# The first feed-forward product by Strassen's method, two tiles at a time, from tile 8 on

## The chip, the cores and the metric

The kernel runs on one core of a Trainium2 chip. The metric is the device time in microseconds of one execution. The engines are named as in the profile: PE is the matrix engine (PEld its weight loads), DVE, ACT and POOL are the vector, scalar and general-purpose engines, and SP issues the DMAs. PE reads its operands from SBUF and writes into PSUM banks of 128 partitions by 512 float32.

## The reference

Banded attention of 8 batches, 8 heads, 576 positions and 64 features per head, then a normalized feed-forward layer of width 512 to 2048 to 512 with a residual:

```python
# heads 0..3: the last 32 keys; heads 4..7: every 4th of the last 128 keys
scores = np.where(masks[None, :, :, :], scale * np.matmul(q, k.transpose(0, 1, 3, 2)), -1000000000.0)
attn = np.exp(scores - np.max(scores, axis=-1, keepdims=True))
attn = attn / (np.sum(attn, axis=-1, keepdims=True) + 1e-09)
x = np.matmul(attn, v).transpose(0, 2, 1, 3).reshape(B, S, H * D)  # (8, 576, 512)
xn = (x - mu) / np.sqrt(var + 1e-06) * g_ln
out = x + np.maximum(xn @ w_ch1, 0.0) @ w_ch2
```

The weights come as float64, everything else as float32.

## The kernel before

The 4608 rows are 36 tiles (`NT`) of 128 rows. Attention is computed a tile at a time: L loads q, k and v, A (`attn_prep`) splits them into float16 halves, S (`attn_scores`) makes the two sets of scores on PE and masks them on DVE, M (`attn_softmax`) makes the softmax on DVE, POOL and ACT and turns the probabilities round by 32-square DVE transposes (`to_columns`), V (`attn_values`) multiplies by the values on PE and leaves the tile's result `x`. N (`norm`) normalizes `x` and splits it into a high and a low float16 half, `xh` and `xl` (L568, L569); T (`transposes`) turns both round by two DMA transposes issued from SP (L576). Tiles 0 to 3 (`EARLY`) take another route through attention, in float32, while the weights are still being loaded and converted.

Every float32 product of the feed-forward is made of three float16 products: high by high, high by low, low by high. The first product, "up" (`up`, L597), has 128 by 128 pieces of `w_ch1` as the stationary operand and the transposed `x` as the moving one. Per chunk of 128 hidden features that is 4 pieces of the depth of 512, times 3, 12 matmuls. ACT takes the relu of the bank as the high half `hh` (L603), and DVE makes the low half `hl` (L604). The second product, "down" (`down`, L620), has 128-column pieces of `hh` and `hl` as the stationary operand and 512 columns of `w_ch2` as the moving one, 48 matmuls a tile, cut into four parts of 12. After the fourth, DVE adds the residual (L626) and SP stores the tile.

Blocks are of `NB` = 3 tiles. The first two blocks (`APART`) run up a tile at a time, with 128 moving columns; from tile 6 on, up has 384 moving columns for three tiles at once, 192 matmuls a block. There are two copies of the transposed `x` (`xT`), used in turns, so that T of a block may run while up of the block before it still reads.

The order of work is a list of units with due times: `unit` gives each its time, not earlier than those of the units it names as having to come first, and the list, sorted by time, is the order in which the program is written down. From there the framework orders the instructions of each engine along a simulated time line (`schedule_with_timeline_sim=True`); those inside `tc.high_priority()` go ahead of others that are ready. At run time each engine goes through its own list in order. For tiles that are not early, the due time of A is `start - AHEAD - PER_TILE * ...`, where `start` is when the block's up is due. `MOVED` puts single units at other times by hand. In each pool, a buffer is given out again once its last reader is done: `ps_f` has 4 banks, `slot` has `SLOTS` = 5 buffers (raw weights, q and k of every other tile, and the split q and k of each tile).

Of the kernel before, what the change touches and what calls it, by code (L numbers as in the profile page):

```python
# [32 lines left out]
NBLK = NT // NB  # L33
EARLY = 4
AHEAD = 64.3
GAP = 17.2
SOFTMAX, VALUES, READY = 0.9, 23.0, 21.7
LOAD = -12.6
PER_TILE = 21.7
CW, SLOTS = 2, 5  # L40
HG = 4
SUMS = 128
# [6 lines left out]
    "U": (42.0, 66.0, 84.0), "D": 106.0, "v": 70.0, "X": 84.0, "t": (88.0, 112.0),  # L49
# [9 lines left out]
}  # L59
APART = 2  # L60
# [8 lines left out]
def attention_then_ffn(ctx: ExitStack, tc, qkv, masks, g, w1, w2, out):  # L69
# [33 lines left out]
    for i in range(NV):  # L103
# [4 lines left out]
    w1_sb = const.tile([P, NKC + 1, NKC, DM], F32, name="w1_sb")  # L108
    w1_16 = w1_sb.bitcast(F16).rearrange("p q c (a f) -> p q c a f", a=2)
    xT = [  # L110
        const.tile([P, 2, NKC, NB * P], F16, name="xT"),
        w1_16[:, NKC].rearrange("p c a f -> p (c a f)")[:, 0 : 2 * NKC * NB * P].rearrange(
            "p (a c n) -> p a c n", a=2, c=NKC
        ),
    ]


    w2_sb = const.tile([P, NFC, DM], F32, name="w2_sb")
    def w2_f32(f, n):
        x, at = (w2_sb, f + 4) if f < NFC - 4 else (w1_sb[:, NKC], f - NFC + 4)  # L120
        return x[:, at : at + n]
# [3 lines left out]


# [43 lines left out]
    def load_tile_now(t):  # L170
        if t == 0:
            state["early"] = work.tile([P, 2, 2, HP, P], F32, name="qk32", bufs=1)
# [4 lines left out]
        else:  # L177


            if t % 2:  # L180
                qk32 = slot().bitcast(F32).rearrange("p (a x h c) -> p a x h c", a=2, x=2, h=HP)
            else:
                qk32 = work.tile([P, 2, 2, HP, P], F32, name="qk32", bufs=1)
# [70 lines left out]
    def room_of(t):  # L254

        st = state[t]
        x = slot().bitcast(F16)
        at = 0
        for name, *shape in (("qs", H, P), ("khp", HP, W + P), ("klp", HP, W + P), ("khd", HP, P), ("kld", HP, P), ("vl", H, D)):
            n = shape[0] * shape[1]  # L260
            st[name] = x[:, at : at + n].rearrange("p (h c) -> p h c", h=shape[0])
            at += n

# [197 lines left out]
    def values_early(t):  # L461
# [21 lines left out]
        x = work.tile([P, 2, HP, D], F32, name="x", bufs=2 * NB + 1)  # L483
# [47 lines left out]
    def to_x(t, pv, scale):  # L531
# [7 lines left out]
        x = work.tile([P, 2, HP, D], F32, name="x", bufs=2 * NB + 1)  # L539
# [5 lines left out]
    def norm(t):  # L545
# [9 lines left out]
        xn = work.tile([P, DM], F32, name="xn", bufs=1)  # L555
# [10 lines left out]
        xh = work.tile([P, DM], F16, name="xh")  # L566
        xl = work.tile([P, DM], F16, name="xl")
        nc.scalar.copy(xh, xn)  # L568
        nc.gpsimd.tensor_tensor(out=xl, in0=xn, in1=xh, op=ALU.subtract)  # L569
        st.update(xh=xh, xl=xl)  # L570

    def transposes(t, blk, i):
        st = state[t]
        blk["xTh"], blk["xTl"] = xT[blk["b"] % 2][:, 0], xT[blk["b"] % 2][:, 1]
        for name, src in (("xTh", st["xh"]), ("xTl", st["xl"])):
            nc.sync.dma_start_transpose(out=blk[name][:, :, i * P : (i + 1) * P], in_=src)  # L576


    def ffn(blk, apart):

        n = NB
        hs = [None] * (NFC // HG)

        def up(fs, i0, i1):

            cols = slice(i0 * P, i1 * P)
            z = ps_f.tile([P, 512], F32, name="ps_f")
            z = z[:, 0 : len(fs) * (i1 - i0) * P].rearrange("p (f n) -> p f n", f=len(fs))
            for n, f in enumerate(fs):
                fq, fc = f // 4, slice(f % 4 * P, (f % 4 + 1) * P)  # L590
# [322 lines left out]
```

## Time and profile before

| | |
|---|---|
| time, median of 3 runs | 942.48 us (940.19 to 942.51) |
| span of the profiled execution, first to last instruction | 942.2 us |
| mean granted PE clock over the span | 0.985 |
| first up (tile 0) | at 58.3 us |
| last matmul of tile 5's up, the last with 128 moving columns | at 231.2 us |
| last block: down of tiles 30 to 32, up, and down of tiles 33 to 35 | 844.99 to 938.36 us |

The page gives the span of the profiled execution and no separate time for it; the span is 0.3 us from the median of the timed runs. The last three entries are starts of matmuls in the trace. The lines of the profile stand in the prediction, each where it is used. In a line of groups, "x1152 | 345.0, 380" means 1152 instructions, 345.0 us of the engine's time in total and 380 ns from start to end of one; matmuls overlap, so their rate is read from the starts of a run of them, or from the chain of work that ended last, which cuts overlapping pieces at the next one's start.

### The profile page before, as it was taken

To read this page: it belongs to the slowest core of one execution; us is meant where nothing else is said; L and a number is where in the kernel's file an instruction comes from. 1 tells how busy PE (TensorE), PEld (TensorE's weight loads), DVE (VectorE), ACT (ScalarE), POOL (GpSimd) and SP (SyncE) were. 2 spreads that over 40 slices of the span, in tenths; PEclk is the share of its full clock that TensorE was granted. 3 is DMA by queue.
4 is the path that set the end of the run, shared out by engine and by line. 5 is a ranking of instruction groups with operands and counts; after the bars stand their busy time and mean duration, and the time that the engine had idled before them with its cause. 6 is when DMAs were issued, how large, how long until landed. Compare 5 with 4: busy or idle time off the path is not lost.

```text
span 942.2 us, 18610 instructions
## 1 busy us (share of the span) xinstructions
PE 890.7 (95%) x7608; PEld 552.2 (59%) x7608; DVE 634.2 (67%) x1379; ACT 312.7 (33%) x588; POOL 312.3 (33%) x319
## 2 busy tenths in 40 slices
PE   4479789999999999999999999999999999999998
PEld 4379466777665555565565565565565565564553
DVE  4799658896977577786686686686686685660210
ACT  4556742334323343251241451241241341130110
POOL 1010273646234235454253353354243341120000
PEclk9979899999999999999999999999999999999999
DMA  7887872754344516446143654364043411010000
GB/s 241 311 229 229 187 176 50 153 122 115 66 75 93 148 52 133 92 71 136 37 80 71 169 105 71 89 123 90 30 88 69 87 27 37 21 24 23 12 1 34
DMA packets 79622, 93.39 MB, mean 99 GB/s; under 512 B 47920, under 2 KB 53680, under 8 KB 79536
## 3 DMA queue, kind: packets, MB, share of 16 engines
q1 hardware_dynamic: 79536, 92.21, 42.3%
q8 instruction: 59, 0.97, 0.4%
q14 instruction: 27, 0.22, 0.1%
HBM read 71.86 MB, written 9.44 MB: 86 GB/s over the span
## 4 chain that ended last, share of the span: by engine, by line
PE 81%; DMA 10%; ACT 3%; DVE 3%; issue 2%; SPq 1%; POOL 1%; ACTq 0%; DVEq 0%; POOLq 0%
PE ps_f L597 36%; PE ps_f L620 35%; PE ps_s L330 4%; PE ps_v L528 4%; DMA row<-in_qkv 4%; DMA slot<-in_w 3%; DMA xT<-xl 1%; ACT row L226 1%; DMA slot<-in_qkv 1%; DMA v<-in_qkv 0%; PE ps_f L673 0%; ACT w_sb L153 0%; DVE slot L662 0%; POOL slot L280 0%; DVE slot L154 0%
## 5 line engine op out<-in xcount | busy, mean ns | idle before, releaser
L620 PE MATMUL ps_f<-w_sb,hh 128*128 128x512 f16 x1152 | 345.0, 380 | 5.8 <-ACT w_sb L153 5.0
L597 PEld LDWEIGHTS <-w_sb 128*128 128x128 f16 x3072 | 256.0, 99 | 126.6 <-issue 4.6
L620 PE MATMUL ps_f<-w_sb,hl 128*128 128x512 f16 x576 | 219.1, 380 | 0.0
L597 PE MATMUL ps_f<-xT,w_sb 128*128 128x384 f16 (+1 forms) x1536 | 199.2, 289 | 2.9 <-DMA xT<-xh 2.4
L597 PE MATMUL ps_f<-w_sb 128*128 128x384 f16 (+1 forms) x1536 | 196.7, 287 | 0.0
L620 PEld LDWEIGHTS <-hh 128*128 128x128 f16 x1152 | 111.8, 98 | 131.5 <-issue 6.8
L603 ACT ACTIVATE hh<-ps_f 128x384 f16<-128x384 f32 (+1 forms) x184 | 91.1, 500 | 216.8 <-PE ps_f L597 216.8
L604 DVE SCALAR_TENSOR_TENSOR hl<-ps_f,hh 128x384 f16<-128x384 f32 (+1 forms) x184 | 100.2, 569 | 42.4 <-ACT hh L603 40.3
L620 PEld LDWEIGHTS <-hl 128*128 128x128 f16 x576 | 56.5, 98 | 67.1 <-issue 1.8
L362 DVE TENSOR_TENSOR sc<-ps_s,mask 32x256 f32<-32x256 f32 x128 | 53.6, 419 | 51.2 <-PE ps_s L330 49.8
L435 DVE STREAM_TRANSPOSE pt_d<-pk 32x256 f32<-32x256 f32 x128 | 79.4, 621 | 1.8
L626 DVE SCALAR_TENSOR_TENSOR row<-ps_f,s,x 128x512 f32<-128x512 f32 x36 | 27.0, 749 | 74.5 <-PE ps_f L620 74.0
L446 POOL TENSOR_TENSOR sc<-sc,mx 128x512 f32<-128x512 f32 x32 | 33.4, 1043 | 116.3 <-DVE mx L444 116.3
L451 ACT ACTIVATE p<-sc 128x512 f32<-128x512 f32 x32 | 20.2, 631 | 128.2 <-POOL sc L446 128.2
L569 POOL TENSOR_TENSOR xl<-xn,xh 128x512 f16<-128x512 f32 x36 | 42.0, 1166 | 59.1 <-ACT xh L568 49.8
L330 PE MATMUL ps_s<-slot 128*128 128x128 f16 (+1 forms) x768 | 58.8, 226 | 2.1 <-DVE sc L348 2.1
L330 PEld LDWEIGHTS <-slot 128*128 128x128 f16 x768 | 50.9, 99 | 12.7 <-DVE sc L348 3.0
L287 POOL COPY slot<-slot 128x128 f16<-128x128 f16 x56 | 17.5, 340 | 119.4 <-PE ps_v L528 119.3
L348 DVE TENSOR_TENSOR sc<-ps_s,mask 32x256 f32<-32x256 f32 x128 | 53.5, 418 | 4.9 <-PE ps_s L330 3.4
L453 POOL TENSOR_TENSOR pk<-p,pk 128x512 f16<-128x512 f32 x32 | 40.7, 1271 | 45.8 <-ACT pk L452 45.8
L458 DVE STREAM_TRANSPOSE pt_b<-pk 32x128 f16<-32x128 f16 x87 | 26.1, 300 | 42.0 <-ACT pk L452 28.4
L554 POOL TENSOR_TENSOR rstd<-rstd,mhalf 128x1 f32<-128x1 f32 x36 | 21.1, 587 | 94.9 <-DVE rstd L553 85.2
(100 smaller groups left out, 961.3 us busy)
## 6 DMA issues: line engine op xcount, KB each, us to landing
qk<-in_qkv SPq DMA_DIRECT2D x36, 512.0 KB, 6.9
slot<-in_qkv SPq DMA_DIRECT2D x32, 512.0 KB, 6.7
slot<-in_w SPq DMA_DIRECT2D x14, 1024.0 KB, 6.3
out_x<-row SPq DMA_DIRECT2D x36, 256.0 KB, 2.0
row<-in_qkv SPq DMA_DIRECT2D x33, 256.0 KB, 2.9
v<-in_qkv SPq DMA_DIRECT2D x33, 256.0 KB, 3.0
slot<-in_w SPq DMA_DIRECT2D x4, 512.0 KB, 7.3
slot<-in_qkv SPq DMA_DIRECT2D x28, 64.0 KB, 4.5
```

The lines of the kernel that those rows point to most:

```text
L330: nc.tensor.matmul(out, lhs, rhs, start=(n == 0), stop=(n == len(terms) - 1))
L348: nc.vector.tensor_tensor(out=sc[pj, 0:HP, :], in0=ps[pj, :, W * j : W * j + 2 * W], in1=mask_16[pj, m : m + 1, :].broadcast_to([W, HP, 2 ...
L362: nc.vector.tensor_tensor(out=sc[pj, HP:H, :].rearrange("p h (t i) -> p h t i", t=2), in0=ps[pj].rearrange("p h (t c) -> p h t c", t=2)[:, ...
L435: nc.vector.transpose(dd[pj].rearrange("p t h (i r) -> p r t h i", r=DIL)[:, j], pk[pj, HP:H, :].rearrange("p h (t i) -> p t h i", t=2),)
L446: nc.gpsimd.tensor_tensor(out=sm, in0=sc, in1=mx.broadcast_to([P, H, 2 * W]), op=ALU.subtract)
L453: nc.gpsimd.tensor_tensor(out=pk16[:, :, :, 1], in0=p32, in1=pk16[:, :, :, 0], op=ALU.subtract)
L528: nc.tensor.matmul(oo, l, r, start=(n == 0), stop=(n == len(mm) - 1))
L569: nc.gpsimd.tensor_tensor(out=xl, in0=xn, in1=xh, op=ALU.subtract)
L597: nc.tensor.matmul(z[:, n], l, r, start=(m == 0), stop=(m == len(mm) - 1))
L603: nc.scalar.activation(hh, z, AF.Relu)
L604: nc.vector.scalar_tensor_tensor(out=hl, in0=z, scalar=0.0, in1=hh, op0=ALU.max, op1=ALU.subtract)
L620: nc.tensor.matmul(o, l, r, start=(f == 0 and m == 0), stop=(f == NFC - 1 and m == 2))
```

## The change

From tile 8 (`FIRST`) on, tiles go in pairs. The pair's normalized `x` (256 rows by 512) is cut into quarters: A11 and A12 are the two halves of the depth of the first tile, A21 and A22 of the second. Four sums of quarters are made on POOL at the end of N of the second tile: S3 = A11 - A21, S1 = A21 + A22, S2 = S1 - A11, S4 = A12 - S2. The weights' quarters (256 of depth by 256 of 512 features, for each of the four groups `fg`) are combined once into T1 to T4 (`combine`), on POOL and for T3 on DVE; T4 takes the place of the quarter B12, after tile 7's up. Up of a pair is then seven products of quarters instead of eight, in two halves `s` of the hidden features. Each product is 24 matmuls with 128 moving columns. Products 6, 7 and 4 are added by PE into the bank `u` that holds product 1, product 3 into the bank `f` that holds product 5; the values in between that another result needs are copied out to SBUF by ACT (`copied`) or added to such a copy by DVE (`added`). The relu halves are made as before, two of the four in each half with the low part on POOL.

Tiles 6 and 7 run up a tile at a time, as tiles 0 to 5 do. There is one copy of the transposed `x` and its sums for the pairs, so that T of a pair comes after the last up step of the pair before it, `(4, 1)`; N of a tile comes after T of the tile before. Of the `ORDER` of a pair, a bracket is a product and its half, a string a part of a down ("p3" is the last part of the tile before). The early tiles' q and k, one in four of the raw weights, and some of the float32 weights move into `tw_sb`, where T1 to T3 are put later; q and k of the other tiles go into `slot`, of which there are 4. The lists of hidden halves (`h`) have 12 buffers that are also used for the copies and for `combine`.

```diff
-AHEAD = 64.3
-GAP = 17.2
+FIRST = 8
+KQ = 256
+AHEAD = 58.0
+GAP = 16.5
-PER_TILE = 21.7
-CW, SLOTS = 2, 5
+PER_TILE = 20.7
+CW, SLOTS = 2, 4
+NH = 12
+NX = 5
...
+    xT = const.tile([P, 2 * 7 * 2 * P], F16, name="xT")
+    xT_pair = xT.rearrange("p (a q k n) -> p a q k n", a=2, q=7, k=2)
...
+            add, sub = ALU.add, ALU.subtract
+            for to, x0, x1, op in ((4, 2, 3, add), (5, 4, 0, sub), (1, 1, 5, sub), (2, 0, 2, sub)):
+                nc.gpsimd.tensor_tensor(out=xs[:, to], in0=xs[:, x0], in1=xs[:, x1], op=op)
+            st.update(halves_for_transpose(xs[:, 1:6], 1))
...
+    def evacuate(z, h, on_pool=False):
+        hh, hl = (h[:, a].rearrange("p g n -> p (g n)") for a in range(2))
+        with tc.high_priority():
+            nc.scalar.activation(hh, z, AF.Relu)
+            if on_pool:
+                nc.gpsimd.tensor_scalar(z, z, scalar1=0.0, scalar2=None, op0=ALU.max)
+                nc.gpsimd.tensor_tensor(out=hl, in0=z, in1=hh, op=ALU.subtract)
+            else:
+                nc.vector.scalar_tensor_tensor(out=hl, in0=z, scalar=0.0, in1=hh, op0=ALU.max, op1=ALU.subtract)
...
+        z = f32_tile().rearrange("p (c f) -> p c f", c=2)
+        e = nc.vector if op in ("T3",) else nc.gpsimd
+        e.tensor_tensor(out=z, in0=pieces(x, 0, fg), in1=pieces(y, 0, fg), op=sub)
+        e.tensor_tensor(out=z, in0=z, in1=pieces(x, 1, fg), op=add)
+        e.tensor_tensor(out=z, in0=z, in1=pieces(y, 1, fg), op=sub)
+        hi, lo = pieces(op, 0, fg), pieces(op, 1, fg)
+        nc.scalar.copy(hi, z)
+        e.tensor_tensor(out=lo, in0=z, in1=hi, op=sub)
...
+    PRODUCTS = {
+        1: ("A11", "11"), 2: ("A12", "21"), 3: ("S4", "22"), 4: ("A22", "T4"), 5: ("S1", "T1"), 6: ("S2", "T2"),
+        7: ("S3", "T3"),
+    }
+    def product(n, s, to, start):
+        x, w = PRODUCTS[n]
+        q = QUARTER[x]
+        for j in range(HG):
+            fg, fc = 2 * s + j // 2, slice(j % 2 * P, (j % 2 + 1) * P)
+            for k in range(2):
+                ws = [pieces(w, a, fg)[:, k, fc] for a in range(2)]
+                for m, (l, r) in enumerate(triple(ws, (xT_pair[:, 0, q, k], xT_pair[:, 1, q, k]))):
+                    nc.tensor.matmul(
+                        to[:, j * P : (j + 1) * P], l, r, start=start and j == 0 and k == 0 and m == 0,
+                        stop=j == HG - 1 and k == 1 and m == 2, skip_group_check=not start,
+                    )
...
+        if n == 1:
+            me["u"] = bank()
+            product(1, s, me["u"], True)
+            me["p1"] = copied(me["u"])
+        elif n == 5:
+            me["f"] = bank()
+            product(5, s, me["f"], True)
+            me["p5"] = copied(me["f"])
+        elif n == 6:
+            product(6, s, me["u"], False)
+            me["u2"] = copied(me["u"])
+        elif n == 2:
+            e = bank()
+            product(2, s, e, True)
+            evacuate(added(e, me["p1"]), outcome(0, 0))
+        elif n == 3:
+            product(3, s, me["f"], False)
+            evacuate(added(me["f"], me["u2"]), outcome(0, 1), True)
+        elif n == 7:
+            product(7, s, me["u"], False)
+            evacuate(added(me["u"], me["p5"]), outcome(1, 1), True)
+        else:
+            product(4, s, me["u"], False)
+            evacuate(me["u"], outcome(1, 0))
...
+        do("N", VALUES + 2, norm, f"V{t}", f"T{t - 1}")
+        unit(f"T{t}", t_at + READY, lambda t=t: transposes(t), f"N{t}", *after)
...
+    ORDER = (
+        (1, 0), (5, 0), "p3", (6, 0), (2, 0), (3, 0), (7, 0), (1, 1), (5, 1), (4, 0),
+        (6, 1), (2, 1), (3, 1), (7, 1), "00", (4, 1), "01", "02", "03", "10", "11", "12",
+    )
+    UP, DOWN = 1.35, 2.6
...
+        ups = f"u{t0}.4.1"
+        start = max(start + PER_TILE * 2, when)
```

More of the change, by code (lines that the diff above doesn't have):

```diff
@@ L177, in load_tile_now @@
         else:
[L180 to L183, printed above, removed]
+            qk32 = slot().bitcast(F32).rearrange("p (a x h c) -> p a x h c", a=2, x=2, h=HP)
             src = qkv[t, :, 0:NQK].rearrange("(a d) e -> d a e", a=2)
@@ L262, in room_of @@
             at += n
+        st["vl"] = work.tile([P, H, D], F16, name="vl", bufs=NV)
     def attn_prep(t):
@@ L538, in to_x @@
         nc.vector.reciprocal(rs, rs)
[L539 removed]
+        x = work.tile([P, 2, HP, D], F32, name="x", bufs=NX)
         nc.vector.tensor_tensor(
@@ new lines, in down @@
+    def down(t, part, chunks):
+        if part == 0:
+            state["o", t] = bank()
+        o = state["o", t]
+        h = state.pop(("h", t, part))
+        for n, f in enumerate(chunks):
+            hh, hl = h[:, 0, n], h[:, 1, n]
+            for m, (l, r) in enumerate(((hh, w2h[:, f]), (hh, w2l[:, f]), (hl, w2h[:, f]))):
+                nc.tensor.matmul(
+                    o, l, r, start=part == 0 and n == 0 and m == 0, stop=part == 3 and n == HG - 1 and m == 2,
+                )
+        if part == 3:
+            y = work.tile([P, DM], F32, name="row")
+            nc.vector.scalar_tensor_tensor(
+                out=y, in0=o, scalar=state["inv"], in1=state[t]["x"].rearrange("p a h d -> p (a h d)"),
+                op0=ALU.mult, op1=ALU.add,
+            )
+            nc.sync.dma_start(out=out[t * P : (t + 1) * P, :], in_=y)
@@ new lines, in step, with outcome, copied, added @@
+    def step(n, s, t0):
+        me = state.setdefault(("s", t0, s), {})
+        def outcome(i, half):
+            state["h", t0 + i, 2 * s + half] = halves_tile()
+            return state["h", t0 + i, 2 * s + half]
+        def copied(x):
+            z = f32_tile()
+            with tc.high_priority():
+                nc.scalar.copy(z, x)
+            return z
+        def added(x, z):
+            with tc.high_priority():
+                nc.vector.tensor_tensor(out=z, in0=x, in1=z, op=ALU.add)
+            return z
+        if n == 1:
[19 more added lines that the diff above has]
+            evacuate(added(me["u"], me["p5"]), outcome(1, 1), True)
+        else:
+            product(4, s, me["u"], False)
+            evacuate(me["u"], outcome(1, 0))
@@ L645, in to_f32, with chunks_of @@
+    def chunks_of(t, part):
+        if t < FIRST:
+            return range(part * HG, part * HG + HG)
+        s, half = divmod(part, 2)
+        return [4 * (2 * s + j // 2) + 2 * half + j % 2 for j in range(HG)]
     def to_f32(src, dst, ps, weights, start, stop, first=False):
         nw = len(weights)
-        raw = slot().rearrange("p (a c two) -> p a c two", a=nw, two=2)
+        state["raws"] = state.get("raws", 0) + 1
+        raw = slot() if state["raws"] % 4 else tw_sb[:, 2].rearrange("p c f -> p (c f)").bitcast(I32)
+        raw = raw.rearrange("p (a c two) -> p a c two", a=nw, two=2)
@@ L693, in prep_w1 @@
         fs = slice(fg * DM, (fg + 1) * DM)
-        wf = w1_sb[:, fg + 1]
-        ps = ps_f.tile([P, DM], F32, name="ps_f")
+        wf = w1_f32(fg)
+        ps = bank()
         for c in range(0, NKC, CW):
@@ L712, in load_w2 @@
         if f == 0:
-            state["w2_ps"] = ps_f.tile([P, DM], F32, name="ps_f")
+            state["w2_ps"] = bank()
         to_f32(
```

308 lines of the change are left out of this document (157 added, 151 removed), and 4 rows, old and new, of the table MOVED.

## The prediction

> **What bounds the kernel now.** I read the page's shares and slices first, then the busy times by window, then PE's waits.
>
> ```profile
> span 942.2 us, 18610 instructions
> PE 890.7 (95%) x7608; PEld 552.2 (59%) x7608; DVE 634.2 (67%) x1379; ACT 312.7 (33%) x588; POOL 312.3 (33%) x319
> PE   4479789999999999999999999999999999999998
> PEclk9979899999999999999999999999999999999999
> ```
>
> The reader is to see that PE is short of work only in the first six slices (141 us). A busy PE is not yet a full one, so the next views are the windows of 50 and 100 us, then two whole blocks of three tiles, and all waits of PE from 130 us to the end.
>
> ```profile
> 100.00:150.00 50.00, 40.78 (x403) 28.15 (x403) 30.54 (x61) 28.92 (x59) 22.67 (x20) 0.90 0.80 166
> 150.00:200.00 50.00, 48.42 (x616) 35.93 (x614) 41.87 (x97) 19.59 (x31) 33.48 (x33) 1.00 0.48 103
> 200.00:250.00 50.00, 49.86 (x561) 35.01 (x559) 39.72 (x90) 15.72 (x26) 20.61 (x20) 1.00 0.56 120
> 250.00:300.00 50.00, 49.99 (x375) 29.10 (x373) 37.60 (x85) 15.14 (x28) 19.59 (x19) 1.00 0.42 76
> 300.00:400.00 100.00, 96.45 (x742) 55.94 (x741) 69.91 (x165) 35.34 (x70) 38.81 (x39) 0.98 0.45 103
> 569.78:640.09 70.31, 70.31 (x530) 40.92 (x528) 53.53 (x113) 23.75 (x41) 31.22 (x31) 1.00 0.45 87
> 640.09:709.91 69.82, 69.82 (x514) 40.42 (x512) 48.53 (x108) 18.46 (x33) 24.50 (x24) 1.00 0.36 75
> ```
>
> ```profile
> PE ps_v L230 <- DVE x L486: 4.6, 1, 4.6
> PE ps_s L330 <- DVE sc L348: 2.1, 3, 1.0
> PE ps_v L230 <- DVE v_tot L228: 2.1, 1, 2.1
> PE ps_v L528 <- DVE x L540: 1.0, 1, 1.0
> ```
>
> (Columns: length, then busy us of PE, PEld, DVE, ACT, POOL, granted clock, DMA share, GB/s.) From 130 us on PE waits 9.8 us in all. What is missing for a bound by PE is that its busy time is made of matmuls at their full rate, and the next rows show it: the last of the chain of work that ended last, and a stretch of PE's timeline.
>
> ```profile
> 818.92 0.55 PE ps_s L330 x8
> 824.83 0.89 PE ps_s L330 x16
> 838.40 1.23 PE ps_v L528 x40
> 844.99 31.08 PE ps_f L620 x144
> 876.07 31.20 PE ps_f L597 x192
> ```
>
> ```profile
> 229.01 2.40 PE L597 MATMUL ps_f<-w_sb 128*128 128x128 f16 x40
> 231.24 0.59 PE L620 MATMUL ps_f<-w_sb,hh 128*128 128x512 f16 x2
> ```
>
> A down matmul takes 31.08 / 144 = 215.8 ns, an up matmul with 384 columns 31.20 / 192 = 162.5 ns, and attention of a tile 0.55 + 0.89 + 1.23 = 2.67 us. Three tiles: 31.20 + 31.08 + 8.01 = 70.29 us, against blocks of 70.31 and 69.82 us. **PE is full**, and only fewer or cheaper matmuls shorten this stage. With 128 columns, 40 matmuls start in 231.24 - 229.01 = 2.23 us: 55.75 ns each, every one with a weight load of its own.
>
> **The change, part by part.** Up of a pair was 128 matmuls of 384 columns (two thirds of a block): 20.80 us. It becomes 7 products x 2 halves x 24 = 336 matmuls of 128 columns: 336 x 55.75 = 18.73 us. Seven eighths would be 18.20; the rest is the fixed part of more matmuls. That is -2.07 us a pair, and with 14 pairs **-28.9 us**. Tiles 6 and 7 go back to 128 columns: 2 x 192 x 55.75 = 21.41 for 20.80, **+0.6 us**. Downs and attention keep their matmuls: a pair then lasts 18.73 + 8 x 2.59 + 2 x 2.67 = 44.8 us, where 46.9 stand now.
>
> A rule of the Trainium skill speaks against the first term: "TensorE: Matmul & The Clock Gate", section "Back-to-back issue gap", says that in a real stream of weight loads and matmuls one at 128 columns takes about 81 ns and one at 512 about 131 ns. By it the seven products would take an estimated 336 x 81 = 27.2 us, 6.4 us a pair more than now and some 90 us in all. The trace disagrees at both ends, with 55.75 and 215.8 ns.
>
> What the other engines get must fit beside 44.8 us of PE. Their rows, and one place where an evacuation stood behind other work:
>
> ```profile
> L604 DVE SCALAR_TENSOR_TENSOR hl<-ps_f,hh 128x512 f16<-128x512 f32 x24 | 16.3, 685 | 3.1 <-ACT hh L603 2.7
> L603 ACT ACTIVATE hh<-ps_f 128x512 f16<-128x512 f32 x24 | 14.2, 593 | 30.5 <-PE ps_f L597 30.5
> L540 DVE TENSOR_TENSOR x<-ps_v,rs 128x512 f32<-128x512 f32 x32 | 22.1, 691 | 1.0
> L308 ACT CAST slot<-qk 128x1024 f16<-128x1024 f32 x16 | 16.7, 1045 | 49.6 <-PE ps_v L528 40.9 <-POOL slot L280 8.6 <-DMA qk<-in_qkv 0.2
> L569 POOL TENSOR_TENSOR xl<-xn,xh 128x512 f16<-128x512 f32 x36 | 42.0, 1166 | 59.1 <-ACT xh L568 49.8 <-issue 9.2
> L287 POOL COPY slot<-slot 128x128 f16<-128x128 f16 x56 | 17.5, 340 | 119.4 <-PE ps_v L528 119.3
> ```
>
> ```profile
> 530.66 0.30 DVE L458 STREAM_TRANSPOSE pt_b<-pk 32x128 f16<-32x128 f16 x1 [0.48 <-POOL pk L453]
> 530.86 0.49 ACT L603 ACTIVATE hh<-ps_f 128x384 f16<-128x384 f32 x1 [0.86 <-PE ps_f L597]
> 535.69 1.49 DVE L604 SCALAR_TENSOR_TENSOR hl<-ps_f,hh 128x384 f16<-128x384 f32 x3
> ```
>
> ACT: six copies and eight relus of 0.59 us for 10.7 relus of 0.49 (the relu of 384 columns below), and a longer cast, about +3.5 us on 16: 43% of a pair. DVE: six sums of 0.69 and four low parts of 0.69 for 10.7 of 0.50 (1.49 / 3), about +1.5 us on the 32 to 36 of a pair now (two thirds of the blocks): up to 83%. POOL: four low parts, each a maximum that the trace doesn't show (0.34 us by the copy of 128 columns, at most 1.17 like a subtraction) and a subtraction of 1.17; four sums of quarters at half of 1.17; a split of 1280 columns where one of 512 was (+1.75). That is 10 to 13.5 us on 16 to 21: up to 76%. None of them becomes the bound; on average PE hides all of it. The price lies in the order, as each engine keeps its list.
>
> **New waits.** PE adds into a bank that ACT or DVE must have read first. Product 6 waits for the copy of product 1 (cover: product 5 and "p3", or two products), 7 for the copy of u (two products), 4 for DVE's sum of u and p5 (two products, or "00"). A product is 24 x 55.75 ns = 1.34 us, so the shortest cover is 2.6 us, and copy or sum take 0.6 to 0.7 when the engine is free: 1.9 us are to spare. Before, a finished bank had three more banks, some 5.8 us, as spare. Queued behind a waiting matmul stand all of PE's products and downs, and the ACT and DVE work that they release. The rows above show what can use up the spare: the relu ended at 531.35, and its low half began at 535.69, 4.3 us later, behind the 5.0 us in which DVE turns round one tile's probabilities. There are two such stretches a pair, 10 of 44.8 us, and two sums that product 4 waits for: 0.45 meetings a pair if they fall by chance; the sum is then late by between 0 and 5.0 - 1.9 us, on average 0.96 (3.1 squared, halved, over 5.0): 0.43 us a pair, **+6 us**. Ends: 0, if the list is written with the sums ahead, and 3.1 us a pair, one full meeting in each. I take the chance value, since the row shows a low half behind the stretch although it has high priority.
>
> **The single xT.** T of a pair now waits for (4, 1) of the pair before. On SP, the loads of the tile after and the stores stand behind it. Its transposes on SP when nothing else moves, and the DMA's work on them:
>
> ```profile
> 844.38 1.19 SPq L576 DMA_TRANSPOSE w_sb<-xh  x1
> 845.66 1.22 SPq L576 DMA_TRANSPOSE w_sb<-xl  x1
> 847.00:848.00 1.00, 1.00 (x6) 0.48 (x5) 0.00 (x0) 0.00 (x0) 0.00 (x0) 1.00 0.58 113
> 848.00:849.00 1.00, 1.00 (x7) 0.46 (x5) 0.00 (x0) 0.00 (x0) 0.00 (x0) 1.00 0.00 0
> xT<-xl SPq DMA_TRANSPOSE x18, 5.9
> ```
>
> Two of 512 columns and two of 1280 (each 1.2 us if the width costs nothing, 3.05 in proportion): 4.9 to 8.5 us of SP, and from the end of the last issue 1.1 us (848.0 - 846.88) to 4.7 (5.9 - 1.2): 6 to 13 us. Six parts of downs (15.5 us), a tile's attention (2.7) and product 1, which needs the first tile only (1.3), cover 19.5 us. Hidden; without cover it would be 6 to 13 us a pair. The first pair has three parts of downs after tile 7's up, 11.8 us in all, while `combine` runs T4 on POOL: 0 to 5 us. The early part also loses a `slot` and gains 12 combinations on POOL (4 x 1.17 us each: 56 us, where 96 of 200 us are busy from 100 to 300 us) and 4 on DVE; PE's 3.5 idle us after 300 could go, or some 10 be added where tiles 4 to 9 come late. First pair and early part together: **+2 us**. Smaller rings of `x` and hidden halves hold what lives at once (four of 5, eight of 12): nothing.
>
> **Sum:** 942.2 - 28.9 + 0.6 + 6 + 2 = 921.9, and the median of the timed runs is 0.3 above the span: **922 us**.
>
> **Rivals.**
> 1. Sums behind the transposes in every pair (the other side). The order repeats with the pair, so it may be met always or never. Place: DVE, ahead of product 4. From 28.9 - 0.6 - 2 = 26.3 us of gain, 26.3 / 14 = 1.9 us a pair decide; one full meeting, 3.1 us, gives 916 + 43 = 959. For: the 4.3 us above, DVE at 83%. Against: PE has no such wait now, and other downs can be listed ahead of a late product. At half of this, 1 to 1.9 us a pair, 930 to 942.
> 2. N of the second tile is written down behind (4, 1), since it follows T of the first. If it also runs there: 4 x 0.58 + 2.9 us on POOL, a cast of 1.3 (1045 ns for 1024), the transposes, 2 us of statistics, together 16 to 20 us against 19.5, and SP's other issues between: up to 3 us in 13 pairs, 916 + 39 = 955. Against: its engines have room, and by the due times its input is ready some 16 us before (4, 1).
> 3. The weight load bounds the narrow matmuls. A load lasts 98 ns by the row below; 336 of them in a row would be 32.9 us a pair, 12.1 more than up now, and add 170 us. Against: 40 pairs of load and matmul in 2.23 us, and runs of 48 at 55.8. The page's 81 ns leads to the same side.
> 4. The early part slips by 10 us or more: 930 to 940.
> 5. The waits never bite, and the 3.5 idle us go: 908 to 912.
>
> ```profile
> L620 PEld LDWEIGHTS <-hh 128*128 128x128 f16 x1152 | 111.8, 98 | 131.5 <-issue 6.8
> 190.69 2.68 PE ps_f L597 x48
> ```
>
> **How the numbers follow.** Forecast, 912 to 930: 0.58. Rival 5: 0.05. Rival 1 at half: 0.15, in full: 0.09. Rival 2: 0.07. Rival 3: 0.02. Rival 4: 0.04. The range runs from 908 to 943 and leaves out rival 2, 3 and the full rival 1, 0.18 in all. A measurement tells 0.3% (2.8 us) from no change: faster, under 939.6, are the forecast, rival 5, rival 4 and most of the half rival 1, 0.78; within, 0.06; slower, 0.16.
>
> **What would show it.** In the profile after: product matmuls starting each 55.8 ns, 48 in 2.68 us; a pair of about 45.2 us between 300 and 900 us; the maximum on POOL between 0.34 and 1.17 us; PE's waits for the copies and for the sum of u and p5 at about 6 us. Wrong would be PE waits for DVE's sums or for xT of over 1.9 us a pair, product matmuls at 80 to 100 ns, or idle PE between 150 and 300 us.

## The result: slower by 2.6 per cent, and the profile after

| | before | after |
|---|---|---|
| median of the timed runs, us (the 942.48 above is that of the first three runs before) | 941.88 (940.19 to 942.51, 4 runs) | 966.3 (963.84 to 968.5, 4 runs) |
| ratio after / before | | 1.0262, 95% interval 1.024 to 1.0283 |
| span of the profiled execution, us | 942.2 | 964.8 |

The forecast was 922 us with a range up to 943: wrong, and on the wrong side. Three lines of the page of the kernel after (the span, the engines' shares, PE's slices) come first:

```profile
span 964.8 us, 25246 instructions
PE 877.8 (91%) x10776; PEld 655.8 (68%) x10776; DVE 656.0 (68%) x1383; ACT 373.1 (39%) x648; POOL 573.7 (59%) x535
PE   5398598998889998999999979999999999999998
```

PE's busy time fell from 890.7 to 877.8 us, yet the span grew by 22.6: PE now stands idle for 87 us where it was idle for 51.5. Before, every slice from the seventh to the last but one was a 9; now there are 8s, most of them between 145 and 300 us, where idle PE was one of the prediction's signs of being wrong, and a 7 at 555 to 579 us. The windows of the kernel after (columns as before: length, busy us of PE, PEld, DVE, ACT, POOL, granted clock, DMA share, GB/s) say where:

```profile
100.00:150.00 50.00, 38.25 (x393) 27.12 (x392) 31.23 (x71) 33.40 (x68) 21.32 (x20) 0.86 0.52 118
150.00:200.00 50.00, 44.73 (x504) 32.18 (x503) 42.22 (x85) 14.54 (x23) 39.52 (x38) 0.93 0.38 85
200.00:250.00 50.00, 44.20 (x528) 32.26 (x526) 42.66 (x79) 17.85 (x31) 40.06 (x35) 1.00 0.45 92
250.00:300.00 50.00, 45.77 (x611) 36.47 (x610) 34.31 (x76) 14.55 (x22) 29.41 (x28) 0.97 0.28 68
300.00:400.00 100.00, 95.20 (x1147) 69.42 (x1144) 69.10 (x157) 43.56 (x78) 70.15 (x65) 1.00 0.46 102
```

From 200 to 300 us PE had 0.15 us idle before and has 10.03 now. No engine is full there: POOL is at 80% at most, DVE at 85%. That points at the order of work more than at the load, which the experiments have to show. The largest waits of PE, first from 100 to 305 us, then from 305 us (the first Strassen product starts at 305.5) to the end:

```profile
PE ps_f L652 <- ACT w_sb L161: 8.9, 1, 8.9
PE ps_v L536 <- DVE pt_a L442: 6.1, 3, 2.7
PE ps_v L536 <- DVE x L548: 5.1, 2, 3.3
PE ps_s L338 <- POOL slot L317: 2.0, 1, 2.0
```

```profile
PE ps_v L536 <- DVE pt_a L442: 9.8, 11, 1.6
PE ps_s L338 <- DVE sc L356: 5.2, 8, 2.3
PE ps_f L652 <- DVE h L627: 4.4, 2, 2.5
PE ps_f L700 <- ACT h L715: 1.9, 2, 1.0
PE ps_f L700 <- DMA xT<-xh: 1.4, 1, 1.4
PE ps_f L700 <- DMA xT<-xl: 0.7, 1, 0.7
```

In the kernel before, the two largest from 100 to 305 us, and then all from 305 us:

```profile
PE ps_f L620 <- ACT w_sb L153: 5.0, 1, 5.0
PE ps_v L230 <- DVE x L486: 4.6, 1, 4.6
```

```profile
PE ps_v L230 <- DVE v_tot L228: 2.1, 1, 2.1
PE ps_s L330 <- DVE sc L348: 0.5, 1, 0.5
```

Each row is: the waiting instruction, what it waited for, us in all, times, the longest. L536 is the values product of attention (V), L338 the scores (S), L652 the downs, L700 the seven products; in the kernel before, L620 is the downs, L330 the scores and L230 the scale of the values. The new waits that the prediction priced stand in the last three rows of the kernel after, 4.0 us in all. The large ones are at V and S, **in attention, whose matmuls and softmax the change did not rewrite**; 4.4 us more are a down's wait for a low half. The 8.9 us for the converted weights (`w_sb`) are mostly not new; they were 5.0 before.

**The books.** Waits alone don't show short losses. So for each matmul I took the time from its start to the next start and subtracted its time at full rate. That rate follows from the 55.75 ns (128 columns) and 215.8 ns (512 columns) of the prediction: (215.8 - 55.75) / 384 = 0.417 ns a column, plus 2.4 ns a matmul. What is left over is "lost" PE time (a lower granted clock is in it, as from 150 to 200 us, 0.93 where it was 1.00; and the extra time of the float32 matmuls of the first tiles counts as lost in every version), in us:

| | 0 to 100 us | 100 to 305 | 305 to end | of the last: ahead of V | ahead of S |
|---|---|---|---|---|---|
| before | 44.1 | 19.8 | 4.7 | 0.1 | 0.7 |
| after | 44.8 | 38.9 | 35.3 | 14.3 | 7.6 |
| difference | +0.7 | +19.1 | +30.6 | +14.2 | +6.9 |

The losses grew by 50.4 us. The arithmetic promised -28.9 + 0.6 = -28.3. The sum, +22.1, is within 0.5 us of the 22.6 by which the span grew. So the question is not whether Strassen saved its eighth, but what the 50 us are.

**The saving itself is there.** Two lines of PE's timeline of the kernel after, each 24 matmuls of a product:

```profile
737.95 1.50 PE L700 MATMUL ps_f<-xT,w_sb 128*128 128x128 f16 x24
739.29 1.50 PE L700 MATMUL ps_f<-xT,tw_sb 128*128 128x128 f16 x24
```

739.29 - 737.95 = 1.34 us for 24, 55.8 ns each, as forecast. The rule of the Trainium skill that spoke against it ("TensorE: Matmul & The Clock Gate", "Back-to-back issue gap", 81 ns at 128 columns) doesn't hold in this stream either. From the first product of one pair to that of the next, the kernel after takes 46.83, 48.83, 50.11, 46.2, 46.8, 53.6, 47.42, 46.25, 46.44, 46.28, 46.13, 46.38 us, and 41.9 for the last, which has less attention in it. The first twelve take 47.6 on average. 44.8 was forecast without waits; two tiles took 46.9 before.

### The profile page after: what moved, and what is told of

Its sections match the earlier page's. It is cut to its first block, busy times and chain, and to the rows that moved or that the text cites. A ratio compares the mean times of both kernels' runs of the same rounds, so it can differ in the third digit from the quotient of the medians.

```text
span 964.8 us, 25246 instructions
## 1 busy us (share of the span) xinstructions
PE 877.8 (91%) x10776; PEld 655.8 (68%) x10776; DVE 656.0 (68%) x1383; ACT 373.1 (39%) x648; POOL 573.7 (59%) x535
## 4 chain that ended last, share of the span: by engine, by line
PE 32%; DVE 17%; POOL 15%; issue 5%; ACT 4%; DMA 3%; POOLq 0%; ACTq 0%; DVEq 0%; SPq 0%
PE ps_f L652 17%; PE ps_f L700 11%; DVE pt_d L443 4%; POOL slot L288 4%; POOL slot L317 3%; PE ps_s L338 3%; DVE pt_a L440 2%; POOL pk L461 2%; DVE sc L356 2%; DVE pt_a L442 2%; DMA row<-in_qkv 2%; PE ps_v L536 2%; POOL h L624 2%; POOL sc L454 1%; DVE h L720 1%
## 5 line engine op out<-in xcount | busy, mean ns | idle before, releaser
L652 PE MATMUL ps_f<-w_sb,h 128*128 128x512 f16 x1728 | 394.2, 382 | 16.2 <-ACT w_sb L161 8.9
L652 PEld LDWEIGHTS <-h 128*128 128x128 f16 x1728 | 166.1, 99 | 201.2 <-issue 19.7
L700 PE MATMUL ps_f<-xT,w_sb 128*128 128x128 f16 x2688 | 167.9, 219 | 0.0
L700 PEld LDWEIGHTS <-w_sb 128*128 128x128 f16 x2688 | 155.8, 98 | 7.4
L624 POOL TENSOR_SCALAR h<-h 128x512 f32<-128x512 f32 x56 | 83.3, 1495 | 126.1 <-ACT h L622 126.0
L700 PE MATMUL ps_f<-xT,tw_sb 128*128 128x128 f16 x2016 | 127.5, 219 | 4.0 <-ACT h L715 1.9
L700 PEld LDWEIGHTS <-tw_sb 128*128 128x128 f16 x2016 | 117.3, 98 | 7.2 <-issue 4.5
L637 PE MATMUL ps_f<-xT,w_sb 128*128 128x128 f16 x1536 | 100.5, 228 | 4.7 <-DMA xT<-xh 4.4
L622 ACT ACTIVATE h<-h 128x512 f16<-128x512 f32 x84 | 51.5, 627 | 110.4 <-DVE h L720 110.4
L595 POOL TENSOR_TENSOR xl<-xs,xh 128x512 f16<-128x512 f32 (+1 forms) x36 | 63.9, 1776 | 35.7 <-ACT xh L594 35.7
L288 POOL TENSOR_TENSOR slot<-slot 128x512 f16<-128x512 f32 x64 | 75.9, 1201 | 2.3
L317 POOL TENSOR_TENSOR slot<-slot 64x1024 f16<-64x1024 f32 x32 | 69.1, 2159 | 11.6 <-ACT slot L316 7.6
L338 PE MATMUL ps_s<-slot 128*128 128x128 f16 (+1 forms) x768 | 58.4, 226 | 9.2 <-DVE sc L356 6.9
L625 POOL TENSOR_TENSOR h<-h 128x512 f16<-128x512 f32 x56 | 66.1, 1192 | 0.5
L370 DVE TENSOR_TENSOR sc<-ps_s,mask 32x256 f32<-32x256 f32 x128 | 53.6, 419 | 16.2 <-PE ps_s L338 14.7
```

The source lines that it names most:

```text
L288: nc.gpsimd.tensor_tensor(out=lo, in0=x32, in1=hi, op=ALU.subtract)
L317: nc.gpsimd.tensor_tensor(out=qsv[D:P], in0=st["q32"][D:P], in1=qsv[D:P], op=ALU.subtract)
L338: nc.tensor.matmul(out, lhs, rhs, start=(n == 0), stop=(n == len(terms) - 1))
L370: nc.vector.tensor_tensor(out=sc[pj, HP:H, :].rearrange("p h (t i) -> p h t i", t=2), in0=ps[pj].rearrange("p h (t c) -> p h t c", t=2)[:, ...
L595: nc.gpsimd.tensor_tensor(out=xl[:, 0:m], in0=x, in1=xh[:, 0:m], op=ALU.subtract)
L624: nc.gpsimd.tensor_scalar(z, z, scalar1=0.0, scalar2=None, op0=ALU.max)
```

## The experiments

All but the last two are one profiled execution each, beside a run of the kernel before on the same chip (940 to 944 us); they are read by their lost time as above and by their waits more than by the last microsecond. Thirteen executions of the kernel before, taken beside the last two, spread from 936.85 to 947.83 us, so a few us between two single times show nothing. The first 100 us differ from version to version by some microseconds (40.8 to 47.3 us lost) though no edit is meant for them, so a difference there is not counted for an edit.

### Is it POOL's load, or the sums of weight quarters?

POOL has the largest rise, 312.3 to 573.7 us busy. The low parts of products 3 and 7 went back to DVE (**e1**):

```
-            evacuate(added(me["f"], me["u2"]), outcome(0, 1), True)
+            evacuate(added(me["f"], me["u2"]), outcome(0, 1))
-            evacuate(added(me["u"], me["p5"]), outcome(1, 1), True)
+            evacuate(added(me["u"], me["p5"]), outcome(1, 1))
```

> All four low parts of a half are made by DVE, none by POOL: per pair POOL loses 4 maxima of 1.50 us and 4 subtractions of 1.19 us (10.8 us), DVE gains 4 x 0.69 us (2.8 us). Theory POOL (the added POOL work makes the softmax chain late, and PE stands at the values product): the PE waits before the values matmuls between 310 and 900 us fall from some 16 us to under 5, and the time falls by 10 to 20 us from 966. Rival DVE (PE waits because DVE has too much ahead of what PE needs): the waits grow, and the time rises by 5 to 10 us.

969.05 us. POOL's busy time from 310 to 900 us falls from 404.7 to 273.1 us, DVE's rises from 418.6 to 448.4, and nothing is won: V loses 20.4 us now (14.3 in after), S 11.7. The theory that PE waits for POOL's load fails, as far as this edit tests it: it gives DVE 30 us more, and V's wait for DVE's `pt_a` after 305 us grows from 9.8 to 14.9 us. With V placed later as in e2 below (**e9**), the same edit gives 960.49, 10 us worse than e2 alone, so there too DVE has less room for this work than POOL.

> e2 and e1 together: values product due at 27 us, all low parts by DVE. POOL falls from 59% to some 44% of the span, DVE rises by 2.8 us a pair. Theory order: POOL's load is not what PE waits for, so the time stays within 5 us of e2's 950.2, and waits of score matmuls for DVE rise. Theory load: with the list no longer ahead, POOL's load is what is left, and the time falls by 8 us or more.

**e3** leaves the sums of weight quarters out: T1 to T4 become plain copies by ACT.

```
-        e.tensor_tensor(out=z, in0=pieces(x, 0, fg), in1=pieces(y, 0, fg), op=sub)
...
-        nc.scalar.copy(hi, z)
-        e.tensor_tensor(out=lo, in0=z, in1=hi, op=sub)
+        nc.scalar.copy(hi, pieces(x, 0, fg))
+        nc.scalar.copy(lo, pieces(x, 1, fg))
```

> Leaves out the sums of weight quarters: each T is a plain copy of its first quarter by ACT (two copies of 512 columns), so 48 POOL and 16 DVE operations of some 1.2 and 0.7 us are gone before 350 us; everything after is the same work. Theory combine (this work delays the attention of tiles 4 to 9): PE's idle time beyond full rate between 100 and 305 us falls from 39 us towards the 19 of the kernel before, time down 12 to 20 us. Rival (the early loss is from the removed hand placements, the missing slot and the third place of xT): under 5 us.

963.59 us, 3 less than after. On top of e2 (**e8**) it gives 946.66 against 950.23. The times are as the rivals had them, and neither difference is larger than the spread of single runs. Stage by stage, the sums matter more than the time says: without them the loss from 100 to 305 us falls by 8.8 us in e3 and by 6.0 in e8, and the loss after 305 us rises by 7.4 and 2.7. So somewhat under half of the 19 us of the early stage goes with the sums, but a large part of it is only lost later instead.

> As e2, without the sums of weight quarters: each T is a plain copy of its first quarter by ACT. PE's time beyond full rate from 150 to 305 us is 15.6 us in e2, 2.6 in the kernel before. Theory combine: it falls to under 6, time down 9 to 13 us from 950.2. Rival (removed hand placements and smaller rings): it stays above 11, time within 5 us.

Putting the sums off in time (**e12**: due time of T1 to T4 116 to 165, with V later; in it T3 of the later groups reads the second quarter after T4 has taken its place, so that part of the weights is another) gives 962.06: what it wins from 100 to 305 us (27.7 lost) it gives back after 305 (43.2), 19.5 of it between 300 and 350 us, where the granted clock was 0.83 and PE busy for 36.41 of 50 us.

> As e2, with the combinations due from 165 us in place of 116. Same work. If they delay the attention of tiles 4 to 7, whose scores and values PE waits for between 130 and 250 us, the loss there (15 us) falls by 4 us or more, and the time to 946 or under. If they only fill room, within 3 us of 950.2.

### Is it where attention stands in PE's list?

`VALUES` is how long after A of the same tile the unit V is due; it was 23 in the kernel before too. **e2** changes that alone:

```
-SOFTMAX, VALUES, READY = 0.9, 23.0, 21.7
+SOFTMAX, VALUES, READY = 0.9, 27.0, 21.7
```

> The due time of the values product is 27 us after the tile's start in place of 23; no work is added or removed. Theory order (POOL and DVE have room, but PE's list holds the values product some 1 us too early for a chain that runs slower than planned): the waits before the values matmuls fall from some 16 us between 310 and 900 us to under 5, time down 8 to 15 us. Theory load (POOL's chain is late however late PE asks): the waits stay within 3 us of what they are, and the time within 4 us of 966.

950.23 us: one number gives 16 us back. V's waits after 305 us fall from 9.8 us to 1.5, as this edit's theory of order had it, while those of S grow:

```profile
PE ps_s L338 <- DVE sc L356: 9.2, 12, 1.3
PE ps_v L536 <- DVE pt_a L442: 1.5, 2, 0.8
```

Two pairs run without a gap. Their windows, in e2:

```profile
586.90:631.80 44.90, 44.90 (x562) 33.52 (x561) 34.67 (x75) 18.54 (x29) 31.52 (x30) 1.00 0.43 100
723.70:768.50 44.80, 44.80 (x561) 33.52 (x560) 34.71 (x75) 18.11 (x29) 30.10 (x28) 1.00 0.42 98
```

By the starts of their first products they last 44.83 us each: **the pair of the prediction, 44.8, exists.** The engines beside PE fit into it with room (DVE 34.7 of 44.8 us, POOL 31). Still, e2 as a whole loses 27.7 us after 305, with S now the largest wait. **e5** goes on in the same direction, `VALUES` 31:

> The values product is due 31 us after the tile's start (27 in e2, 23 in the changed kernel). After e2, 1.5 us of PE waits before values matmuls are left after 305 us, so theory order says: within 4 us of e2's 950.2, the rest lying elsewhere. If the list is still ahead of the real chain, another 5 us or more go. A rise of over 4 us would come from norm and the transposes behind it, as waits of the up steps for xT.

953.51. V loses 2.5 us, but S 19.1; the waits have moved. Its largest after 305 us:

```profile
PE ps_s L338 <- DVE sc L356: 16.1, 9, 5.2
```

Three tries to give that wait room as well, all with `VALUES` 27, moved it too. **e6** makes the second set of scores a unit of its own, 2.5 us after the first: S's waits go from 9.2 to 5.0 us, and the downs' waits for DVE's low half rise to 5.0; 950.88, as e2.

> As e2, with the second set of scores a unit of its own, due 2.5 us after the first, since it goes into the one score bank that DVE reads for 1.7 us after the first. Theory order: the waits before score matmuls (9.2 us after 305 us, 2.8 before) fall to under 3, time down 6 to 10 us from e2's 950.2. Rival (DVE is simply busy when the first set ends): they fall by less than a third, time within 3 us.

**e7** takes the sums of squares of nine tiles' values in four portions, at four tiles, where they were taken at one: the two long pairs shrink from 51.07 and 50.64 us to 48.94 and 49.25, an early wait of 5.8 us appears; 952.43.

> As e2, with the nine squares of v for the next group's scale spread over four tiles (3, 2, 2, 2) in place of all at one. Same work. Theory (ACT's list holds squares that wait for their loads, and the copies that products 6 and 7 wait for stand behind them): the pairs of 48.9 to 51.1 us fall to under 47.5, the waits of product matmuls for ACT's copies (4.0 us) to under 1, time down 5 to 10 us. Rival (those pairs are long for the start of the steady stage, not for the squares): within 3 us.

**e10** puts five early units (S6, S7, S9, S10, V8) back to times by hand: 955.26, no help: the loss from 100 to 305 us stays within about 1 us of e2's.

> As e2, with five of the removed hand placements back (S6, S7, S9, S10, V8 at their times of before). If their removal is what the stage from 150 to 305 us lost (15.6 us beyond full rate in e2, 2.6 before), it falls below 9 and the time by 6 us or more. If the loss is from other parts of the change (the combinations took 3.6 us in e8), it stays within 4 us of 950.2 or rises, since these times were set for another plan.

### Is it what was changed around the products?

**e11** keeps the whole surroundings of the change (four slots, one `xT`, the new rings, due times and `vl` out of the slot), but no pair is ever formed; every up is done a tile at a time with 128 columns:

```
-FIRST = 8
+FIRST = 36
```

> FIRST is 36: no tile goes by Strassen, all run up a tile at a time with 128 columns; smaller rings, one xT of three places, the combinations and the due times (values at 23) stay as in the changed kernel. At full rate tiles 6 to 35 cost 30 x 0.32 us more than before (9.4 us), so 951 without more waits than before. Theory coupling (the seven products, their copies, sums and low parts bring the waits): from 320 us to the end PE loses under 8 us beyond full rate, where the changed kernel loses 33; the time is 960 to 972 with the early loss of 20 us. Rival (rings, xT and due times bring them): it loses 20 us or more there, 975 or above.

983.69 us, span 981.9. The rival's side of the expectation (20 us or more lost late, 975 or above) came. Before, blocks from tile 6 on took 10 x 31.20 = 312.0 us of up; at 128 columns the same 30 tiles take 30 x 10.70 = 321.1, so 942.2 + 9.1 = 951.3 would be its span with the losses of before. It has 30.6 more, and its lost time is up by 30.1: 46.0, 29.0 and 23.7 us in the three stretches. Its waits after 305 us, **with no Strassen product in the program**, lead with the very ones of the kernel after:

```profile
PE ps_v L536 <- DVE pt_a L442: 10.7, 15, 1.1
PE ps_s L338 <- DVE sc L356: 3.3, 7, 0.5
```

Before, the same stretch had 2.1 and 0.5 us (the wait for `v_tot` and one for the scores). By this run some 30 of the 50 us come with the surroundings, and the products add the other 20 (after minus e11: -1.2, +9.9, +11.6) while they save 14 x (21.41 - 18.73) = 37.5 us against e11. Net that is 17.2, and the two spans differ by 17.1. The split is a difference between programs that also list their work differently: from tile 8 on, e11 goes a tile at a time, as neither of the others does, so the 30 us are what this program loses, and not a part that was measured inside the kernel after.

**Which part of the surroundings?** POOL's list shows one suspect. In the groups of POOL, the first copy of a tile's split of q and k (L287 before, L295 after) waited for the values product of an earlier tile before: "119.4 <-PE ps_v L528 119.3" in the prediction's row. In after and in e11 it waits for the scores instead (one row of each, in this order):

```profile
L295 POOL COPY slot<-slot 128x128 f16<-128x128 f16 x56 | 17.5, 342 | 29.1 <-PE ps_s L338 29.1
```

```profile
L295 POOL COPY slot<-slot 128x128 f16<-128x128 f16 x56 | 18.3, 356 | 195.2 <-PE ps_s L338 195.2
```

`vl`, which V reads, no longer lies in the slot; the slot's last reader is now S, so a slot comes free for the split of a next tile right after S, and the split runs there, ahead of this tile's softmax. POOL's timeline, first in the kernel before:

```profile
636.26 2.12 POOL L309 TENSOR_TENSOR slot<-qk,slot 64x1024 f16<-64x1024 f32 x1 [0.22 <-ACT slot L308]
638.47 2.34 POOL L280 TENSOR_TENSOR slot<-qk,slot 128x512 f16<-128x512 f32 x2
640.76 1.15 POOL L569 TENSOR_TENSOR xl<-xn,xh 128x512 f16<-128x512 f32 x1
642.65 1.04 POOL L446 TENSOR_TENSOR sc<-sc,mx 128x512 f32<-128x512 f32 x1 [0.74 <-DVE mx L444]
```

and in the kernel after:

```profile
733.75 1.05 POOL L295 COPY slot<-slot 128x128 f16<-128x128 f16 x2 [4.18 <-PE ps_s L338]
734.90 2.13 POOL L317 TENSOR_TENSOR slot<-slot 64x1024 f16<-64x1024 f32 x1
737.11 2.27 POOL L288 TENSOR_TENSOR slot<-slot 128x512 f16<-128x512 f32 x2
739.34 1.04 POOL L454 TENSOR_TENSOR sc<-sc,mx 128x512 f32<-128x512 f32 x1
```

Before, POOL is idle when DVE's maximum arrives (the bracket) and subtracts at once. After, 5.6 us of split start at 733.75, the maximum ends at 737.98 (737.31 + 0.67, DVE's row below), and POOL is still in the split then: no bracket, the subtraction starts the moment the split is done, at 739.34.

```profile
737.31 0.67 DVE L452 TENSOR_REDUCE mx<-sc 128x8 f32<-128x512 f32 x1
```

Over tiles 12 to 33, the subtraction starts 0.12 us after the end of the maximum before and 3.02 us after it now, on average (2.1 in e11). The values product starts 19 to 20 us after the scores in most tiles before, 21 to 28 after.

Putting `vl` back is no clean test, and **e14** shows why:

```
+        for name, *shape in (..., ("vl", H, D)):
...
-        st["vl"] = work.tile([P, H, D], F16, name="vl", bufs=NV)
```

> Undoes one part: the low half of v lies in the slot of the split q and k again, so that a slot comes free after the values product as before, not after the scores. Theory release (the changed kernel frees the slot one step earlier, the next tile's split then runs between this tile's scores and softmax, and delays the softmax): the first subtraction starts under 2.5 us after the maximum, waits before values fall below 5 us, time down 8 to 18 us. Rival (the split itself becomes late, with 4 slots in place of 5 and a half): score matmuls wait for the split, time 966 or more.

1041.1 us. POOL's copy waits for V again, and the subtraction only 0.82 us, so what frees the slot does set POOL's order. But four slots held until V are too few: POOL's first copies stand 82.7 us for V in all, and PE waits for the transposed `x` (30.2 and 7.2 us):

```profile
PE ps_f L699 <- DMA xT<-xh: 30.2, 9, 6.4
PE ps_v L535 <- DVE pt_a L441: 13.3, 7, 7.7
PE ps_f L699 <- DMA xT<-xl: 7.2, 3, 3.2
```

**e16**, the same with e15's edits below, is at 1023.11 in the same way. With the slots held until V, as before, the four of the change don't do; it could go down to four only because it frees them at S.

> e15 with the low half of v in the slot again (e14). If priority and release act on the same delay, it is within 4 us of e15; if the release also sets when the split comes, the waits of scores show it, and it is slower.

Giving A more lead (**e4**, `AHEAD` 58 to 64.3) doesn't help either: 969.99.

> AHEAD is 64.3 again, so that the attention of a tile is due 6.3 us earlier against the up steps that use it; no work is added or removed. If the softmax chain only lacks lead, the waits before the values and scores matmuls fall by half or more and the time by 8 to 15 us. If PE's list is made by when the planner believes the inputs ready, the lead changes little: within 4 us of 966.

Nor does high priority for the softmax's subtractions and exponentials (**e13**). It left POOL's order as it was (the subtraction waits 3.0 us again) and so doesn't test the theory; of its 8 us (958.22), 4 lie in the first 100 us. (The 0.7 to 0.8 us that its expectation gives for the kernel before are POOL's idle time ahead of the subtraction; from the end of the maximum it is 0.12.) **e15** takes the maximum of products 3 and 7 from POOL to ACT, with `VALUES` 25: 959.76, behind e2, where its theory had 935 to 948.

> Undoes nothing and adds nothing: the softmax's two subtractions on POOL and its two exponentials on ACT get the high priority that the up evacuations have. In the changed kernel POOL's first subtraction starts 2 to 7 us after DVE's maximum (0.7 to 0.8 in the kernel before), with the split of the next tile's q and k (6.5 us of POOL) and the low parts ahead of it. Theory queue (PE waits because that work stands ahead of the softmax in POOL's list): the delay falls to under 2.5 us, the waits before values matmuls after 305 us from 14 us to under 5, the time by 10 to 18 us from 966. Rival load (POOL at 59% is simply late): the waits move to the score and down matmuls, time within 5 us of 966.

> e13, and the maximum of the low parts (1.50 us on POOL, 4 a pair) becomes a relu by ACT (0.6 us), values due at 25 us. POOL loses 6 us a pair, ACT gains 2.4. If POOL's list is what PE waits for, this is the best of the set, 935 to 948; if DVE and ACT are as late, within 4 us of e13 or of e2's 950.

The order can be forced. **e17** lets the split of tile t (its operations on POOL, and its casts on ACT with them) be listed only behind the last softmax subtraction of tile t - 1; **e18** is that with `VALUES` 27. e17's time is the median of 4 runs, e18's of 10.

```
-        prep_stacked(t)
+        with tc.issue_after(state[t - 1]["pk"]) if t > EARLY else nullcontext():
+            prep_stacked(t)
...
-        nc.gpsimd.tensor_tensor(out=pk16[:, :, :, 1], in0=p32, in1=pk16[:, :, :, 0], op=ALU.subtract)
+        st["pk"] = nc.gpsimd.tensor_tensor(out=pk16[:, :, :, 1], in0=p32, in1=pk16[:, :, :, 0], op=ALU.subtract).ins
```

> The changed kernel with one edge more: POOL's split of the next tile's q and k stands in its list behind this tile's second softmax subtraction; nothing else, values due at 23 us. e13 gave priority and POOL's list stayed as it was, so it tested nothing; e14 shortened the delay (mean 3.0 to 0.8 us) but starved the loads of slots. Theory queue: the mean delay of the first subtraction falls from 3.0 to under 1 us, the waits before values matmuls after 305 us from 14 to under 5 us, the time from 966 to 945 to 955. Rival: the waits move to the score matmuls, which need the split, and the time stays above 960.

> e17 with values due at 27 us. If e2 and e17 cure the same wait, the two together are within 4 us of the better of them (945 to 952). If they cure different parts, it is the best of all, 935 to 944.

| | median us | ratio to before, 95% interval | subtraction's wait | lost 0-100 / 100-305 / 305-end | ahead of V / S |
|---|---|---|---|---|---|
| after | 966.3 | 1.0262, 1.024 to 1.0283 | 3.02 | 44.8 / 38.9 / 35.3 | 14.3 / 7.6 |
| e2 (one run) | 950.23 | | 3.39 | 42.6 / 32.5 / 27.7 | 3.4 / 11.2 |
| e17 | 955.57 (953.68 to 957.93) | 1.0125, 1.0065 to 1.0185 | 0.22 | 47.3 / 31.7 / 31.0 | 14.8 / 2.3 |
| e18 | 949.8 (947.08 to 953.85) | 1.0076, 1.005 to 1.0102 | 0.18 | 42.7 / 31.0 / 26.7 | 0.0 / 0.6 |

POOL's timeline in e17, the subtraction now ahead of the split (not all rows of the stretch):

```profile
751.63 1.05 POOL L455 TENSOR_TENSOR sc<-sc,mx 128x512 f32<-128x512 f32 x1
754.71 1.28 POOL L462 TENSOR_TENSOR pk<-p,pk 128x512 f16<-128x512 f32 x1
756.07 2.46 POOL L318 TENSOR_TENSOR slot<-slot 64x1024 f16<-64x1024 f32 x1
```

e17 brings POOL's wait back to 0.22 us and takes 10.7 us off the time (the ratio goes from 1.0262 to 1.0125): where the split stands was a cause. But V's loss stays at 14.8 us. The theory that POOL's late subtraction makes V wait falls in that form: with the subtraction on time, V simply comes sooner after S (20 to 21 us in most tiles), and PE still stands there, 10.4 us in 12 waits. What e17 wins is S (7.6 to 2.3) and 7.2 us between 100 and 305. V needs the later due time, and with both cures e18 has no loss at V or S to speak of. Its waits after 305 us:

```profile
PE ps_f L701 <- ACT h L716: 5.8, 4, 2.2
PE ps_f L701 <- DVE h L721: 5.8, 8, 1.4
PE ps_f L653 <- POOL h L626: 4.6, 7, 0.7
PE ps_f L653 <- DVE h L628: 2.2, 2, 1.9
PE ps_f L701 <- DMA xT<-xh: 2.1, 1, 2.1
```

Now the products wait for their copies and sums (11.6 us), which is the wait that the prediction had priced; in the kernel after it was 1.9. That attention's waits had covered it there is likely, and not shown. And e18 is no faster than e2, within the spread: curing POOL's order takes 10.7 us off at `VALUES` 23 and hardly anything at 27. In e2, e6, e7 and e18 the lost time after 305 us is 27.7, 25.9, 28.3 and 26.7 us, although PE waits for something else in each. These are the four lowest with pairs: the other versions with `VALUES` at 27 or 31 lose 30 (e8), 32 (e10), 34 (e5), 37 (e9) and 43 us (e12).

## Why the prediction was wrong, point by point

- **What bounds the kernel** (PE is full, only fewer or cheaper matmuls shorten the stage): right, and it hid the danger. With PE full to the last 0.1 us, the other engines had only been shown to keep up at 46.9 us per two tiles, not at 44.8.
- **The product term**, -28.9 us: right. 55.8 ns a matmul, and pairs of 44.83 us where nothing waits. Rival 3, by which the weight load would bound the products, is out.
- **The load of the others** ("None of them becomes the bound; on average PE hides all of it. The price lies in the order"): the loads were right (POOL 70.15 of 100 us, at most 76% forecast; DVE 69.1, at most 83% forecast), though the maximum, which I bounded by 0.34 and 1.17 us, takes 1.495. The sentence about the order was right too. But I looked for that price only at the places that the change writes new, the sums of the products and `xT`, and put nothing on attention, where PE lost 21.1 us more at V and S after 305 us.
- **New waits**, +6 us at the products: 1.9 us in the kernel after, 11.6 in e18 once attention is out of the way. The mechanism exists; as the cause of the result it is small, and the term was too large by 4.1 us for this kernel.
- **The single `xT`**, hidden: 2.1 us of waits, about right. The wide transposes cost hardly more than narrow ones on SP (below).
- **"Smaller rings of `x` and hidden halves hold what lives at once …: nothing", and the lost `slot` within +2 us: the step that failed.** It asked only whether the buffers are enough, and not what the rings and the due times do to the order of attention. What surrounds the products loses 30 us without any product (e11). Moving `vl` out of the slot, which the prediction doesn't mention, changed what frees the slot, from V to S, and with it the order on POOL: the split of the next tile went ahead of this tile's softmax. That the split's place costs is shown by e17, 10.7 us at `VALUES` 23. That V is listed too soon for the chain of the changed kernel is shown by e2, 16 us from one due time; the two overlap, since e18 with both is no faster than e2.
- **First pair and early part**, +2 us: the loss between 100 and 305 us grew by 19.1, 6 to 9 of it with the sums of weight quarters. Rival 4 said "10 us or more" and gave it 0.04. It came, but with attention after 305 us on top, 21 us at V and S, which no rival had. Rivals 1 and 2 (DVE's sums in each pair, N behind (4, 1)) ended on the right side by mechanisms that the waits don't show: the sums aren't among PE's larger waits in after.

What stays open: why even the best versions lose 26 to 28 us after 305 us (4.7 before), at S, at the downs or at the products in turn. The wait moves with each edit, and the sum doesn't fall below that. Nothing is full and pairs without a gap occur, so the cause may lie in how the list fits the chip's real times in the other pairs; but no run isolates it. Of e11's 30 us, the ring of slots, the single `xT` and the due times were not told apart either, apart from POOL's order. No version tried is faster than the kernel before: the best timed one, e18, is at 1.0076 of it, and e8, which leaves work out, was 5.2 us above its neighbour run.

## What to carry to other kernels

When the bounding engine is full and gets less work, every other chain must be shown to keep the new pace, the untouched ones first: here PE lost more at attention than at the new products. A buffer that moves changes what frees it, and what is freed sooner is also issued sooner, on an engine that works through its list in order; so ask of each changed ring what now runs earlier and in front of whom. And when a cure moves a wait to the next instruction without changing the sum, count lost time by stage, since the list of waits alone will look like progress each time.

## What the runs showed of the hardware that was not expected

On POOL, a maximum with one input and a constant takes longer than a subtraction with two inputs of the same size. Two rows of the groups of the kernel after:

```profile
L624 POOL TENSOR_SCALAR h<-h 128x512 f32<-128x512 f32 x56 | 83.3, 1495 | 126.1 <-ACT h L622 126.0
L625 POOL TENSOR_TENSOR h<-h 128x512 f16<-128x512 f32 x56 | 66.1, 1192 | 0.5
```

1495 against 1192 ns. Where one follows the other without a gap, their starts are 1.45 and 1.12 us apart, so it is not an effect of where a span ends; and the softmax's subtraction, which like the maximum writes float32, takes 1.04 us in the rows of POOL above. The Trainium skill, "GPSIMD Engine Reference", "Elementwise — side-by-side cycle accounting", has two inputs as the dearer case, because both share one read port; the rows go the other way for this pair of operations.

A DMA transpose of 1280 columns costs SP little more than one of 512. SP's queue in the kernel after, a narrow one and then the wide one of the pair's second tile:

```profile
713.30 1.24 SPq L610 DMA_TRANSPOSE xT<-xl  x1
728.49 1.33 SPq L610 DMA_TRANSPOSE xT<-xl  x1
```

Of the prediction's bounds, 1.2 us and 3.05 in proportion to the width, the lower one was nearly right.
